# Three edits to an attention and two-MLP kernel: an operand in PSUM, planner slack for weight sums, a shorter attention stretch

## The chip, the cores and the metric

The kernel runs on one core of a Trainium2 chip. Five queues work side by side there: PE (matrix products into eight PSUM banks), DVE (VectorE), ACT (ScalarE), POOL (GpSimd) and SP, which here only issues DMAs. The metric is the device time of one execution in microseconds; lower is better.

## The reference

Windowed attention (4 batches, 8 heads, 576 positions, head size 64), then a gated MLP (width 1536), then an MLP (width 2048), over 2304 tokens of width 512, in fp32:

```python
scores = np.where((rel >= 0) & (rel < 128), q @ k.T / 8 + bias, -1e9)     # per head
attn = softmax(scores) @ v                                               # x: 2304 x 512
g, val = x @ w_gate, x @ w_val
x2 = (silu(g) * val) @ w_out                                             # first MLP
h = x2 @ moe2_w_in
out = silu(h) @ moe2_w_out                                               # second MLP
```

## The kernel before

**Tiles and parts.** The 2304 tokens are three parts of 768. A part is six tiles of 128 tokens, in two blocks of three (N = 384 columns). Each part goes through attention, the first MLP (`moe1`, six groups of 256 hidden units) and the second one (`moe2`, eight groups). PE does the MLPs without a break, first and second MLP of part 0, then part 1, then part 2; the attention of a part lies under the MLPs of the part before it. Inputs and weights are split into a high and a low fp32r half, and a product is three passes (high by high, high by low, low by high), at lines 902 to 904 for the way in (`quad`, seven Strassen products X, Y, Z over 2 x 2 blocks) and 1182 to 1184 or 1212 to 1214 for the way out (`out1`, `out2`).

**The operand of an MLP.** `operands` makes the seven Strassen operands of an input in `XOP`, slots 0 to 6. Its source is `XST` (from attention) or `ACC` (the first MLP's result). Slot 0 (A11) is block 0, columns 0 and 1 of the source. Slots 5, 6, 1 and 4 (S1, S2, S3, S4 and sums of them) come from differences t1 to t4 that `less` writes to PSUM banks. t1 is block 1 minus block 0, and t2 (slot 6, the S2 of the second product) needs t1. `split` writes the high half with a copy (`copy_op`, line 348 on ACT, 349 on DVE) and the low half with a subtraction (`sum_op`, line 357 on DVE, 358 on POOL). If the source is a PSUM bank, the subtraction can only go to DVE.

**The out-sums.** `out1` of group g adds PE's bank to ACC on DVE (line 1196) and gives the bank back. In the last group the block b = 0 comes last, columns d = 0, 1, 2, 3.

**Weight sums in the background.** Part 2 takes Strassen sums of the out-weights as well. `out_sums` makes them during part 1, in 11 jobs (one a group, where there is room): for each of two weights it loads the high half into `word` and the low half into the one buffer `top`, adds them (the word sum, 22 in all), forms four sums (`strassen_sums`, tiles `sums`), splits them (`split_weight`, tiles `later_raw`) and stores them. Part 2 loads them back into tiles `later_...`, some of which take the place of attention's buffers.

**What sets the order.** Every operation goes to a planner (`Plan.add`) with a cost for each engine that can do it, a due time, and what it reads and writes. `Plan.issue` then simulates the engines: an operation is ready when those before it end plus a hand-over time, and each engine takes, of those ready, the one with the earliest due time. This gives each engine a fixed list of instructions, which the chip executes strictly in that order. So an instruction that waits holds up all behind it in its list. `spread` gives attention's tiles their due times: over a stretch `span`, tile by tile. `WLEAD` is how far ahead weights are loaded. Out-weights go through a ring of three buffers `wo0` to `wo2`, two a group, so that the second load of a group waits until the group before has read its first weight for the last time.

Of the kernel before, what the change touches and what calls it, by code (L numbers as in the profile page):

```python
# [56 lines left out]
class Plan:  # L57
# [19 lines left out]
    def add(self, engine, cost, due, fn, reads=(), writes=(), take=None, give=None, port=False, other=()):  # L77
        n = len(self.ops)
        preds = set()
        for key in reads:  # L80
            if key in self.writer:
                preds.add(self.writer[key])
            self.readers.setdefault(key, []).append(n)
        for key in writes:
            if key in self.writer:
                preds.add(self.writer[key])
            preds.update(self.readers.pop(key, ()))
            self.writer[key] = n
        preds.discard(n)
        if isinstance(take, Bank):  # L90
            take = (take,)
        ways = {e: (c, f, p or e == "pool", d) for e, c, f, p, d in [(engine, cost, fn, port, 0.0), *other]}
        self.ops.append((ways, due, preds, take, give))

    def issue(self):
# [25 lines left out]
        def start(e, n, now):  # L121
            ways, _, _, take, _ = ops[n]
            if ways[e][2]:
                now = max(now, port_free)
            if take is not None:
                m = len(take)
                if len(self.banks) < m or any(used[k] + m > self.limits[k] for k in kinds(take[0])):
                    return None
                now = max(now, heapq.nsmallest(m, self.banks)[-1][0])
            if len(ways) > 1 and min(ways, key=lambda o: done(o, n)) != e:  # L130
                return None
            return now
# [27 lines left out]
        while left:  # L160
# [6 lines left out]
            ways, due, _, take, give = ops[n]  # L167
# [25 lines left out]
            for m in succs[n]:  # L193
                for o in ready_at[m]:
                    ready_at[m][o] = max(ready_at[m][o], end + handover(o, e))
                missing[m] -= 1
                if not missing[m]:
                    offer(m)
# [3 lines left out]
def attention_moe_moe2_kernel(  # L202
# [144 lines left out]
    def copy_op(n, due, out, src, reads, writes, give=None, psum=True):  # L347
# [4 lines left out]
            other=[("dve", cost("dve", n), dve, not psum, 500.0)],  # L352
        )

    def sum_op(n, due, out, x, y, op, reads, writes, give=None, psum=False):
# [5 lines left out]
        else:  # L361
            plan.add(
                "pool", cost("pool", n), due, pool, reads, writes, give=give,
                other=[("dve", cost("dve", n), dve, True, 500.0)],
# [309 lines left out]
    def operands(src, name, due, plain=True):  # L674
# [5 lines left out]
        def block(j, blk, kk):  # L680
            c = 2 * j + kk
            return (
                lambda: src[:, blk * BT:blk * BT + BT, c, :],
                [(name, blk * BT + t, c) for t in range(BT)],
            )
# [16 lines left out]
        for kk in range(2):  # L702
            t1[kk] = less(b[0, 1, kk], b[0, 0, kk])
# [58 lines left out]
    def split_weight(dst, key, src, reads, n, due, old=()):  # L762
        out = dst if callable(dst) else lambda: dst
        copy_op(n, due, lambda: out()[:, 0], lambda: src, reads, [key, *old], psum=False)
        sum_op(n, due, lambda: out()[:, 1], lambda: src, lambda: out()[:, 0].bitcast(F32), ALU.subtract, reads, [key])
# [22 lines left out]
    def strassen_sums(a, due):  # L788
        def add(x, y, op):
# [3 lines left out]
            sum_op(2 * P, due, lambda: t, lambda: xa, lambda: ya, op, xk + yk, [tk])  # L793
# [62 lines left out]
    def out_sums(kind, g, due, behind):  # L856
# [14 lines left out]
        for n, (t, tk) in enumerate(strassen_sums(a, due)):  # L871
            m = take("stage", len(STAGE))
            u, uk = STAGE[m][0], ("stage", m)
            split_weight(u, uk, t, tk, 2 * P, due, before.pop(uk, ()))
# [297 lines left out]

    def out1(g, ws, d, blk, hs, due):
# [19 lines left out]
        if g == 0:  # L1193
# [36 lines left out]
    WLEAD = 19050.0  # L1230
    pend = []
# [139 lines left out]
    spread(2, state["t"] + 6000.0, M1 + M2 - 8000.0)  # L1371
# [47 lines left out]
```

## Time and profile before

| | us |
|---|---|
| median of 3 runs | 941.37 |
| lowest, highest | 935.42, 941.68 |
| the profiled execution | 937.67 |
| its span, first to last instruction | 936.0 |
| PE busy in it | 907.9 |
| DVE, POOL, ACT busy | 708.9, 559.6, 531.0 |

All columns of the section of rows are in microseconds from the start of the span, or microseconds of duration, unless a mean is given in ns. In a timeline a row is start, duration, engine, line, instruction and tiles (written <- read), and in brackets the idle time of the engine ahead of it and what ended it. A group of instructions has its count, then busy us, mean ns, then idle time ahead and what ended it. Buffer numbers are left out of tile names. PE's durations are modelled and overlap: a matmul of 512 columns is shown with 0.39 us where the next starts 0.23 us later.

### The profile page before, as it was taken

Reading aid. Unit: us, or ns where it says so; the run is one execution under the profiler, and the core shown is the slowest. Engines: PE = TensorE matmul, PEld = TensorE weight load, DVE = VectorE, ACT = ScalarE, POOL = GpSimd, SP = SyncE. Lnnn points to the kernel's source line nnn. Section 1 sums busy time; section 2 is a strip of 40 time slices with the busy share of each in tenths; the row PEclk is TensorE's granted clock in tenths of the full one; section 3 lists DMA queues with packets and bytes.
Section 4 is the critical chain, followed back from the end, with each engine's and each line's share of the span. In section 5 each row is a group of like instructions: output and inputs, shape, how many; then the busy total and the mean of one; then the engine's idle time right before and its main releaser. Section 6 shows DMA issues by size and latency. Waiting matters only on the chain.

```text
span 936.0 us, 17803 instructions
## 1 busy us (share of the span) xinstructions
PE 907.9 (97%) x5758; PEld 843.8 (90%) x5758; DVE 708.9 (76%) x1602; ACT 531.0 (57%) x1361; POOL 559.6 (60%) x635
## 2 busy tenths in 40 slices
PE   7999999998999999999999999999999999999998
PEld 5799999997888888989999988888799999999996
DVE  7888879879889788647565867667755776778875
ACT  6887567757877675664343575445355333474431
POOL 2865468777657678785524487754144445876453
PEclk9999999999999999999999999999999999999999
DMA  9988997996897987999877789988498888678702
GB/s 222 281 243 258 283 324 221 294 313 206 274 304 260 305 290 265 354 314 304 279 219 244 242 292 330 312 284 311 151 329 249 251 253 253 201 234 245 218 23 91
DMA packets 181677, 241.58 MB, mean 258 GB/s; under 512 B 68048, under 2 KB 97232, under 8 KB 181584
## 3 DMA queue, kind: packets, MB, share of 16 engines
q1 hardware_dynamic: 181584, 240.44, 80.0%
q8 instruction: 46, 0.75, 0.3%
q14 instruction: 47, 0.39, 0.1%
HBM read 169.61 MB, written 70.78 MB: 257 GB/s over the span
## 4 chain that ended last, share of the span: by engine, by line
PE 69%; DVE 12%; DMA 7%; POOL 4%; ACT 4%; issue 3%; SPq 0%; DVEq 0%; POOLq 0%; ACTq 0%
PE bank L902 13%; PE bank L904 12%; PE bank L903 12%; PE bank L1212 4%; PE bank L1214 4%; PE bank L1213 4%; PE bank L607 3%; PE bank L493 3%; PE bank L1182 2%; PE bank L1184 2%; PE bank L1183 2%; DVE word L755 2%; DMA top<-kept_o 2%; PE bank L1118 1%; PE bank L1120 1%
## 5 line engine op out<-in xcount | busy, mean ns | idle before, releaser
L902 PE MATMUL bank<-XOP,wu 128*128 128x384 f32 (+1 forms) x868 | 297.3, 343 | 11.6 <-DVE tmp L963 4.3
L903 PE MATMUL bank<-XOP,wu 128*128 128x384 f32 (+1 forms) x868 | 288.9, 333 | 2.5 <-POOL XOP L358 1.9
L904 PE MATMUL bank<-XOP,wu 128*128 128x384 f32 (+1 forms) x868 | 288.9, 333 | 0.0
L902 PEld LDWEIGHTS bank<-XOP,wu 128*128 128x128 f32 x868 | 163.1, 188 | 23.0 <-ACT tmp L348 8.2
L903 PEld LDWEIGHTS bank<-XOP,wu 128*128 128x128 f32 x868 | 163.3, 188 | 4.4 <-POOL XOP L358 2.1
L904 PEld LDWEIGHTS bank<-XOP,wu 128*128 128x128 f32 x868 | 163.0, 188 | 0.1
L358 POOL TENSOR_TENSOR h<-tmp,h 128x384 fp32r<-128x384 f32 x77 | 81.7, 1071 | 62.0 <-ACT h L348 60.9
L348 ACT ACTIVATE tmp<-bank 128x384 f32<-128x384 f32 x133 | 62.1, 488 | 52.8 <-PE bank L904 28.2
L1026 DVE SCALAR_TENSOR_TENSOR tmp<-tmp,bank 128x384 f32<-128x384 f32 (+1 forms) x120 | 64.4, 542 | 36.4 <-ACT tmp L1015 24.4
L1212 PE MATMUL bank<-wo,h 128*128 128x512 f32 (+1 forms) x218 | 87.3, 401 | 1.7 <-DMA wo<-kept_o 1.7
L1214 PE MATMUL bank<-wo,h 128*128 128x512 f32 (+1 forms) x218 | 85.6, 393 | 0.0
L1213 PE MATMUL bank<-wo,h 128*128 128x512 f32 (+1 forms) x218 | 85.6, 393 | 0.0
L553 POOL TENSOR_TENSOR cs<-cs,st 128x512 f32<-128x512 f32 x36 | 39.9, 1109 | 65.8 <-DVE st L550 44.7
L1224 DVE TENSOR_TENSOR ACC<-bank,ACC 128x512 f32<-128x512 f32 (+1 forms) x97 | 64.1, 678 | 15.4 <-PE bank L1214 14.6
L358 POOL TENSOR_TENSOR wu<-word,wu 128x256 fp32r<-128x256 f32 x63 | 51.1, 824 | 39.4 <-ACT wu L348 35.2
L348 ACT ACTIVATE h<-tmp 128x384 fp32r<-128x384 f32 x97 | 49.5, 523 | 41.9 <-PE bank L1213 20.0
L1182 PE MATMUL bank<-h,wo 128*128 128x384 f32 (+1 forms) x216 | 72.5, 336 | 0.1
L1183 PE MATMUL bank<-h,wo 128*128 128x384 f32 (+1 forms) x216 | 71.5, 331 | 0.1
L1184 PE MATMUL bank<-h,wo 128*128 128x384 f32 (+1 forms) x216 | 71.4, 330 | 0.0
L1015 ACT ACTIVATE tmp<-bank 128x384 f32<-128x384 f32 (+1 forms) x121 | 57.0, 482 | 25.0 <-PE bank L904 11.5
L755 DVE SCALAR_TENSOR_TENSOR word<-raw,top 128x512 int32<-128x512 int32 x68 | 60.9, 895 | 11.7 <-ACT top L752 9.6
L948 DVE TENSOR_TENSOR bank<-bank,tmp 128x384 f32<-128x384 f32 x93 | 52.1, 561 | 22.1 <-PE bank L904 20.3
(414 smaller groups left out, 2149.6 us busy)
## 6 DMA issues: line engine op xcount, KB each, us to landing
wu<-kept_i SPq DMA_DIRECT2D x112, 256.0 KB, 3.5
wu<-kept_g SPq DMA_DIRECT2D x72, 256.0 KB, 4.2
wu<-kept_v SPq DMA_DIRECT2D x72, 256.0 KB, 4.3
wo<-kept_o SPq DMA_DIRECT2D x34, 512.0 KB, 4.7
raw<-in_moe_w_out_dram SPq DMA_DIRECT2D x28, 512.0 KB, 4.9
kept_o<-wo SPq DMA_DIRECT2D x28, 512.0 KB, 4.4
kept_i<-wu SPq DMA_DIRECT2D x56, 256.0 KB, 4.5
kept_s<-later_raw SPq DMA_DIRECT2D x44, 256.0 KB, 4.8
```

The lines of the kernel that those rows point to most:

```text
L348: act = lambda: nc.scalar.activation(out(), src(), AF.Copy)
L358: pool = lambda: nc.gpsimd.tensor_tensor(out(), x(), y(), op)
L755: lambda: nc.vector.scalar_tensor_tensor(w.bitcast(I32), word, 13, top, ALU.logical_shift_right, ALU.bitwise_or),
L902: nc.tensor.matmul(ps, wh, xh, start=start, stop=False, skip_group_check=True)
L903: nc.tensor.matmul(ps, wh, xl, start=False, stop=False, skip_group_check=True)
L904: nc.tensor.matmul(ps, wl, xh, start=False, stop=stop, skip_group_check=True)
L1182: nc.tensor.matmul(ps[:, 0:n], wh, h[:, 0], start=(i == 0), stop=False)
L1183: nc.tensor.matmul(ps[:, 0:n], wh, h[:, 1], start=False, stop=False)
L1184: nc.tensor.matmul(ps[:, 0:n], wl, h[:, 0], start=False, stop=(i == 1))
L1212: nc.tensor.matmul(ps, hh, wh, start=(i == 0), stop=False)
L1213: nc.tensor.matmul(ps, hh, wl, start=False, stop=False)
L1214: nc.tensor.matmul(ps, hl, wh, start=False, stop=(i == 1))
```

## The change

There are three edits.

1. **The operand.** Where the last group of `out1` sums block 0, columns 0 and 1, the sum is written back to PE's own bank (line 1200 of the changed kernel) instead of ACC, and the bank is kept (`left`). In `operands` with source ACC, slot 0 and t1 read this bank. t1 waits until slot 0 is split (`x_keys(0, kk)`), and gives the bank back.
2. **The slack.** `Plan.add` takes a `slack`, which is added to the time at which an operation counts as ready. The background sums and their splits get LATE = 4000 ns each; the word sums get none.
3. **The stretch.** The attention of part 2 is spread over M1 + M2 - 28000 ns instead of M1 + M2 - 8000.

```diff
-    def add(self, engine, cost, due, fn, reads=(), writes=(), take=None, give=None, port=False, other=()):
+    def add(self, engine, cost, due, fn, reads=(), writes=(), take=None, give=None, port=False, other=(), slack=0.0):
...
-                    ready_at[m][o] = max(ready_at[m][o], end + handover(o, e))
+                    ready_at[m][o] = max(ready_at[m][o], end + handover(o, e) + ops[m][5])
...
             c = 2 * j + kk
+            if src is ACC and j == 0 and blk == 0:
+                return (lambda b=left[kk]: tiles(b.tile[:, 0:N])), [left[kk]]
...
         for kk in range(2):
-            t1[kk] = less(b[0, 1, kk], b[0, 0, kk])
+            held = src is ACC
+            t1[kk] = less(b[0, 1, kk], b[0, 0, kk], x_keys(0, kk) if held else (), left[kk] if held else None)
...
-        for n, (t, tk) in enumerate(strassen_sums(a, due)):
+        for n, (t, tk) in enumerate(strassen_sums(a, due, LATE)):
             m = take("stage", len(STAGE))
             u, uk = STAGE[m][0], ("stage", m)
-            split_weight(u, uk, t, tk, 2 * P, due, before.pop(uk, ()))
+            split_weight(u, uk, t, tk, 2 * P, due, before.pop(uk, ()), LATE)
...
-        if g == 0:
+        if g == G1 - 1 and b0 == 0 and d < 2:
+            plan.add("dve", cost("dve", n), due, lambda: nc.vector.tensor_tensor(pv(), pv(), acc, ALU.add), keys, [b])
+            left[d] = b
+        elif g == 0:
             copy_op(n, due, lambda: acc, pv, [b], keys, give=b)
...
+    LATE = 4000.0
...
-    spread(2, state["t"] + 6000.0, M1 + M2 - 8000.0)
+    spread(2, state["t"] + 6000.0, M1 + M2 - 28000.0)
```

The rest of the diff hands `slack` through `copy_op`, `sum_op`, `split_weight` and `strassen_sums`. All lists of instructions are planned anew, from the first edit's place in part 0 on. In all, PE's list is as long as before; 19 of the 22 word sums stand on DVE (14 before), and the six low halves of slot 0 in the three hand-overs from ACC stand on DVE instead of POOL.

**DVE, hand-over from ACC in part 0.** L1196 is an out-sum, L693 (L695) a difference t, L357 with XOP a low half. Before, from the out-sum of block 0, column 0 on:

```order
L1196 TENSOR_TENSOR ACC_65<-bank4_132,ACC_65 128x3x128
L357 TENSOR_TENSOR XOP_63<-bank1_129,XOP_63 128x384
L1196 TENSOR_TENSOR ACC_65<-bank6_134,ACC_65 128x3x128
L1196 TENSOR_TENSOR ACC_65<-bank7_135,ACC_65 128x3x128
L1196 TENSOR_TENSOR ACC_65<-bank5_133,ACC_65 128x3x128
L693 TENSOR_TENSOR bank2_130<-ACC_65 128x384
L693 TENSOR_TENSOR bank4_132<-ACC_65,bank2_130 128x384
L448 TENSOR_TENSOR KR_66<-bank3_131,KR_66 128x2x128
L693 TENSOR_TENSOR bank7_135<-ACC_65 128x384
L357 TENSOR_TENSOR XOP_63<-bank4_132,XOP_63 128x384
L693 TENSOR_TENSOR bank5_133<-ACC_65,bank7_135 128x384
L357 TENSOR_TENSOR XOP_63<-bank2_130,XOP_63 128x384
```

After, from the same sum (now L1200) on:

```order
L1200 TENSOR_TENSOR bank4_132<-bank4_132,ACC_65 128x384
L357 TENSOR_TENSOR XOP_63<-bank1_129,XOP_63 128x384
L1200 TENSOR_TENSOR bank6_134<-bank6_134,ACC_65 128x384
L357 TENSOR_TENSOR XOP_63<-bank4_132,XOP_63 128x384
L695 TENSOR_TENSOR bank2_130<-ACC_65,bank4_132 128x384
L357 TENSOR_TENSOR XOP_63<-bank6_134,XOP_63 128x384
L695 TENSOR_TENSOR bank4_132<-ACC_65,bank2_130 128x384
L758 SCALAR_TENSOR_TENSOR word2_98<-raw1_94,top0_95 128x512
L1205 TENSOR_TENSOR ACC_65<-bank7_135,ACC_65 128x3x128
L357 TENSOR_TENSOR XOP_63<-bank4_132,XOP_63 128x384
L695 TENSOR_TENSOR bank7_135<-ACC_65,bank6_134 128x384
L357 TENSOR_TENSOR XOP_63<-bank2_130,XOP_63 128x384
```

The low halves of slot 0 (XOP<-bank4 and XOP<-bank6, third and fifth behind the sum) are new here. The first low half of slot 6 (the second XOP<-bank4) is ninth behind the sum in both lists. A weight conversion (L758, L755 before) has come ahead of it.

**ACT and DVE, first background sum, at the end of part 0's second MLP.** On ACT L1015 (L1018) is a tanh, and L348 with later_raw the high half of a background sum. ACT before:

```order
L348 ACTIVATE tmp2_108<-bank6_134 128x384
L348 ACTIVATE tmp3_109<-bank4_132 128x384
L348 ACTIVATE tmp4_110<-bank5_133 128x384
L348 ACTIVATE KR_66<-bank1_129 128x2x128
L348 ACTIVATE later_raw0_256_4727<-sums_99 128x256
L1015 ACTIVATE tmp2_108<-bank6_134 128x384
L348 ACTIVATE later_raw0_256_4727<-sums_99 128x256
L456 ACTIVATE qts_119<-bank3_131 128x256
L348 ACTIVATE later_raw1_256_4746<-sums_99 128x256
L1015 ACTIVATE tmp4_110<-tmp5_111 128x384
```

ACT after:

```order
L348 ACTIVATE tmp2_108<-bank2_130 128x384
L348 ACTIVATE XST_64<-bank3_131 128x512
L456 ACTIVATE qts_119<-bank4_132 128x256
L348 ACTIVATE KR_66<-bank0_128 128x2x128
L348 ACTIVATE tmp3_109<-bank7_135 128x384
L348 ACTIVATE tmp4_110<-bank5_133 128x384
L456 ACTIVATE qts_119<-bank6_134 128x256
L1018 ACTIVATE tmp2_108<-bank2_130 128x384
L1018 ACTIVATE tmp4_110<-tmp5_111 128x384
L1018 ACTIVATE tmp3_109<-bank5_133 128x384
L1018 ACTIVATE tmp5_111<-bank7_135 128x384
L348 ACTIVATE later_raw1_256_4797<-sums_99 128x256
```

The four tanhs stand ahead of the first high half of a background sum now. On DVE, L948 (L951) adds to Y, L963 (L966) is the c22 that frees Y's bank. Before, the job's second word sum was on POOL, and DVE had:

```order
L948 TENSOR_TENSOR bank4_132<-bank4_132,tmp2_108 128x384
L448 TENSOR_TENSOR KR_66<-bank1_129,KR_66 128x2x128
L1026 SCALAR_TENSOR_TENSOR tmp2_108<-tmp2_108,bank6_134 128x384
L963 TENSOR_TENSOR tmp5_111<-bank4_132,tmp4_110 128x384
L459 SCALAR_TENSOR_TENSOR qts_119<-bank3_131,qts_119 128x256
L948 TENSOR_TENSOR bank5_133<-bank5_133,tmp3_109 128x384
```

After:

```order
L448 TENSOR_TENSOR KR_66<-bank1_129,KR_66 128x2x128
L357 TENSOR_TENSOR word0_96<-word0_96,top0_95 128x512
L459 SCALAR_TENSOR_TENSOR qts_119<-bank4_132,qts_119 128x256
L951 TENSOR_TENSOR bank7_135<-bank7_135,tmp2_108 128x384
L448 TENSOR_TENSOR KR_66<-bank0_128,KR_66 128x2x128
L459 SCALAR_TENSOR_TENSOR qts_119<-bank6_134,qts_119 128x256
L1029 SCALAR_TENSOR_TENSOR tmp2_108<-tmp2_108,bank2_130 128x384
L966 TENSOR_TENSOR tmp5_111<-bank7_135,tmp4_110 128x384
```

The second word sum (word0) has come to DVE, ahead of the additions to Y.

**PE, last out-products of part 1's second MLP.** Of the three passes of a product only the first is shown. From the last product of the group before with wo1 on, before:

```order
L1212 MATMUL bank7_135<-wo1_91,h4_104 128x512
...
L1212 MATMUL bank7_135<-wo2_92,h1_101 128x512
...
L1212 MATMUL bank4_132<-wo0_90,h3_103 128x512
...
L1212 MATMUL bank0_128<-wo0_90,h3_103 128x512
...
L1212 MATMUL bank5_133<-wo0_90,h3_103 128x512
...
L1212 MATMUL bank6_134<-wo0_90,h2_102 128x512
...
L1212 MATMUL bank7_135<-wo0_90,h2_102 128x512
...
L1212 MATMUL bank4_132<-wo1_91,h4_104 128x512
```

After:

```order
L1221 MATMUL bank2_130<-wo1_91,h4_104 128x512
...
L1221 MATMUL bank2_130<-wo2_92,h1_101 128x512
...
L1221 MATMUL bank0_128<-wo0_90,h3_103 128x512
...
L1221 MATMUL bank1_129<-wo0_90,h3_103 128x512
...
L1221 MATMUL bank7_135<-wo0_90,h3_103 128x512
...
L1221 MATMUL bank6_134<-wo0_90,h2_102 128x512
...
L1221 MATMUL bank3_131<-wo0_90,h2_102 128x512
...
L1221 MATMUL bank4_132<-wo0_90,h2_102 128x512
...
L1221 MATMUL bank0_128<-wo1_91,h4_104 128x512
```

Between the last product with the old wo1 and the first with the new one stand 18 matmuls before and 21 after. The weighing of the last attention tile (L607), which stood directly ahead of the first row, is now 75 rows ahead of it.

## Rows read from the trace of the kernel before

**Rows 1.** Page, part 1: busy us (share of span) x instructions.
```profile
PE 907.9 (97%) x5758; PEld 843.8 (90%) x5758; DVE 708.9 (76%) x1602; ACT 531.0 (57%) x1361; POOL 559.6 (60%) x635
```

**Rows 2.** Windows: stretch, length, busy us (x instructions) by engine, clock, DMA share, GB/s.
```profile
220.00:230.00 10.00, 8.36 (x46) 7.54 (x47) 9.78 (x20) 6.87 (x18) 6.39 (x8) 1.00 0.32 77
```

**Rows 3.** Timeline of PE: rows with idle time ahead, two neighbours at 669.
```profile
220.16 0.45 PE L903 MATMUL bank<-XOP,wu 128*128 128x384 f32 x1 [1.87 <-POOL XOP L358]
...
226.79 0.44 PE L902 MATMUL bank<-XOP,wu 128*128 128x384 f32 x1 [0.75 <-ACT tmp L348]
228.83 0.44 PE L902 MATMUL bank<-XOP,wu 128*128 128x384 f32 x1 [0.73 <-DVE tmp L349]
...
419.50 0.44 PE L902 MATMUL bank<-XOP,wu 128*128 128x384 f32 x1 [1.92 <-DVE tmp L963]
...
464.39 0.44 PE L902 MATMUL bank<-XOP,wu 128*128 128x384 f32 x1 [0.24 <-DVE tmp L963]
...
514.80 0.44 PE L902 MATMUL bank<-XOP,wu 128*128 128x384 f32 x1 [0.70 <-ACT tmp L348]
...
539.10 0.44 PE L902 MATMUL bank<-XOP,wu 128*128 128x384 f32 x1 [0.80 <-ACT tmp L348]
...
634.24 0.45 PE L902 MATMUL bank<-XOP,wu 128*128 128x384 f32 x1 [0.42 <-ACT tmp L348]
...
669.06 0.39 PE L1213 MATMUL bank<-wo,h 128*128 128x512 f32 x1
669.29 0.40 PE L1214 MATMUL bank<-wo,h 128*128 128x512 f32 x1
671.42 0.47 PE L1212 MATMUL bank<-wo,h 128*128 128x512 f32 x1 [1.73 <-DMA wo<-kept_o]
```

**Rows 4.** Timelines of DVE and POOL, hand-over from ACC in part 0.
```profile
217.31 1.47 DVE L1196 TENSOR_TENSOR ACC<-bank,ACC 128x384 f32<-128x384 f32 x3
...
220.10 1.40 DVE L693 TENSOR_TENSOR bank<-ACC 128x384 f32<-128x384 f32 x1
...
217.80 6.52 POOL L358 TENSOR_TENSOR XOP<-ACC,XOP 128x384 fp32r<-128x384 f32 x6
```

**Rows 5.** Groups by line and form: busy us, mean ns, idle; L755 from the page.
```profile
L357 DVE TENSOR_TENSOR XOP<-bank,XOP 128x384 fp32r<-128x384 f32 x48 | 25.3, 549 | 0.7 <-ACT XOP L348 0.3
L358 POOL TENSOR_TENSOR XOP<-ACC,XOP 128x384 fp32r<-128x384 f32 x18 | 19.3, 1107 | 1.1 <-ACT XOP L348 1.1
L357 DVE TENSOR_TENSOR word<-word,top 128x512 f32<-128x512 f32 x14 | 12.0, 860 | 27.0 <-DMA top<-kept_o 19.0 <-DMA word<-kept_o 7.2 <-POOL h L358 0.7
L693 DVE TENSOR_TENSOR bank<-ACC 128x384 f32<-128x384 f32 x12 | 9.1, 759 | 0.1
L693 DVE TENSOR_TENSOR bank<-ACC,bank 128x384 f32<-128x384 f32 x12 | 6.7, 554 | 0.2
L755 DVE SCALAR_TENSOR_TENSOR word<-raw,top 128x512 int32<-128x512 int32 x68 | 60.9, 895 | 11.7 <-ACT top L752 9.6
```

**Rows 6.** Timelines of POOL, ACT, DVE: what stood before PE's 419.50.
```profile
415.46 1.30 POOL L358 TENSOR_TENSOR word<-word,top 128x512 f32<-128x512 f32 x1 [2.05 <-DMA word<-kept_o]
...
417.60 0.42 ACT L348 ACTIVATE later_raw<-sums 128x256 fp32r<-128x256 f32 x1 [2.11 <-POOL sums L358]
417.92 0.47 ACT L1015 ACTIVATE tmp<-bank 128x384 f32<-128x384 f32 x1
...
418.90 0.55 DVE L963 TENSOR_TENSOR tmp<-bank,tmp 128x384 f32<-128x384 f32 x1
```

**Rows 7.** Waits over the kernel: total us, times, longest us.
```profile
ACT later_raw L348 <- POOL sums L358: 26.0, 10, 8.2
```

**Rows 8.** The chain that ended last, in order: start, us, what.
```profile
408.14 7.18 DMA word<-kept_o
...
665.52 5.76 DMA wo<-kept_o
```

**Rows 9.** Page, part 6: DMA issues, KB each, median us to landing.
```profile
wo<-kept_o SPq DMA_DIRECT2D x34, 512.0 KB, 4.7
```

## What I predict, and how

> **What bounds the kernel now.** I read the page's busy shares first: TensorE (PE) is busy for 907.9 of 936.0 us [rows 1], at the full granted clock of 2.4 GHz, also in a slice in which it waits [rows 2]. So PE is the bound, its matmuls are untouched by the change, and the change can only be worth what PE waits. Next I went through the slices of 10 us: the startup apart, PE is short of work where the operand of one MLP is turned into the next one's (220 to 230) and where a weight sum was late (410 to 420). Then I took PE's timeline, kept the rows with idle time ahead of them, and looked at what ended each. [Rows 3] holds the larger waits in the stretches that the change touches. Three families are seen there:
>
> - The operand of the second MLP (ACC to XOP), in part 0 at 220.16, 226.79 and 228.83 and in part 1 at 539.10: 1.87 + 0.75 + 0.73 + 0.80 = 4.15 us.
> - Background weight sums at 419.50, 464.39, 514.80 and 634.24: 1.92 + 0.24 + 0.70 + 0.42 = 3.28 us.
> - A weight load, at 671.42: 1.73 us.
>
> These idle times count from a modelled end. By starts, the wait at 671.42 is 2.13 us after the matmul at 669.29, where neighbours start 0.23 us apart (669.06, 669.29): 1.90 us, so each wait costs about 0.17 us more than its row says. All nine together: 9.16 + 9 x 0.17 = 10.7 us, 1.1% of the span. That is nearly all that is to be had from these three edits.
>
> **The operand kept in PSUM.** At each of three hand-overs (one a part) two sums go to PSUM instead of ACC, as long as before. The high halves are then read from PSUM by ScalarE. The two low halves per hand-over move from POOL, 1107 ns each, to VectorE (DVE), 549 ns each; and the two differences t1 have one operand in SBUF instead of two, 554 ns for 759 ns [rows 5]. On DVE that is 2 x 0.55 - 2 x 0.21 = +0.7 us per hand-over; POOL is relieved of 2.2 us.
>
> In part 0 POOL took six low halves in a row, 217.80 to 224.32 [rows 4], and PE's second matmul waited for the second of them, until 220.16. After the change the sum ends, as before, near 216.9 (in [rows 4] the next sums start at 217.31). ScalarE needs 0.5 us and the low half stands third behind the sum on DVE; with DVE's instructions 0.47 us apart (three in 1.47 us, [rows 4]) it ends near 218.4. The first wait shrinks from 1.87 us to about 0.2. But PE then reaches S2 some 1.6 us earlier, and the low half of S2 stands at the same place as before, nine rows behind the sum. Before, it followed a subtraction from two SBUF operands that took 1.40 us at 220.10 while POOL ran [rows 4], and so ended near 222.0. Now I count rows to about 221.3: PE has its products with A11 done by 220.4 and waits some 0.9 us, and about as much again for the second half of S2, since a weight conversion (L755, 895 ns in the mean, [rows 5]) has moved ahead of each. So nearly all of the 1.7 us is lost again within ten products. What remains is that DVE gets to the additions of Y earlier, on which 226.79 and 228.83 hang: half of their 1.48 us. I take -0.9 us for part 0, from -3.4 (all three waits go) to +2.0 (two low halves and two conversions, 2 x 0.55 + 2 x 0.9 = 2.9 us of DVE work ahead of S2, less the 0.85 that the slow subtraction lost against its 0.55). In parts 1 and 2 the first matmuls did not wait for A11, so there is only 0.80 us to win and 0.7 us of DVE work each to pay: -0.4, from -0.8 to +1.4. Sum of this edit: **-1.3**.
>
> The banks held longer cost nothing that I can find: each waits for a split that takes about 1.5 us, while PE works on out-sums of other banks.
>
> **The slack.** The wait at 419.50 can be followed in [rows 6]: a word sum waited on POOL for a load that took 7.18 us [rows 8]; then came the Strassen sums, and ScalarE stood at 417.60 before a high half of such a sum. Right behind it in the same queue was the tanh for PE's next bank (417.92), then DVE's c22 (418.90), then PE. Over the kernel ScalarE stood so for 26.0 us [rows 7]. With 4 us added to every step the planner puts these instructions behind the tanhs, as the order of ScalarE shows. But the word sum itself has no slack and now stands on DVE, right ahead of the work on Y. That queue waits for the same load, until 408.14 + 7.18 = 415.32 [rows 8]. From there: 0.86 for the sum (mean, [rows 5]); then two instructions of 384 columns at 0.47 and three of 256, by width 0.31; then c22, 0.55: 418.6 against 419.45 (418.90 + 0.55, [rows 6]). The first wait shrinks by 0.8 only. The other three (1.36 + 3 x 0.17 = 1.9) stand behind sums and halves that are delayed, and I let 1.8 of it go. Against this, 19 of the 22 word sums are now on DVE instead of 14; 14 of them had 27.0 us of idle time before them [rows 5], 1.9 each, so DVE idles about 10 us more. Little of such idle time reached PE so far (the 0.24 at 464.39 is the clear case), so +0.4. Sum: **-2.2**, from -4.0 to +5 (if half of those 10 us reached PE).
>
> **The shorter stretch.** The same attention work of the last part is done by 20 us earlier (28000 for 8000 ns off the span). It adds no instruction. PE did not wait for its result: at 676 there is no wait in the operand of part 2. But it changes the order at the end of part 1. There wo1 is loaded when its last reader is through, at 665.52, and lands 5.76 us later [rows 8]; PE had 18 matmuls of 0.23 us to do meanwhile and stood 1.73 us. The change leaves 21: 0.7 us. The 34 such loads land in 4.7 us in the median [rows 9], 1.1 less than this one. With 0.7 + half of 1.1: **-1.2**, from -1.9 (all) to +1 (the load now stands in SP's queue behind a store of the last weight sums, which the slack has made later).
>
> **Sum.** -1.3 - 2.2 - 1.2 = -4.7 us. The profiled execution took 937.67 us: 933.0. It lies 3.7 us under the median of the three runs (941.37) and 2.3 over the lowest, so the runs of one kernel differ by as much as I forecast.
>
> **A rule weighed against the rows.** In [rows 5] the subtraction with two SBUF operands takes 759 ns, that with one 554: 0.2 us lost to POOL's presence. The Trainium skill, SBUF — State Buffer, section Who interferes with whom, says that a VectorE instruction with two SBUF inputs and a GpSimd instruction that reads SBUF exclude each other for a whole instruction, and that one with at most one SBUF input doesn't. The 1.40 us at 220.10 agrees. By the rule the six t1 would escape up to one GpSimd instruction each, an estimate of 6 x 1.1 = 6.6 us of DVE's time by the durations here; if the two in part 0 stood on PE's path, the sum would be 931.2 for 933.0. By the rows it is 6 x 0.2 = 1.2 us, which the +0.7 per hand-over above holds already, and I keep to that. Another rule speaks against the change: by the Trainium skill, PSUM — Partial Sum Buffer, section The four PSUM rules, GpSimd cannot touch PSUM at all, so that the planner has no way to give these low halves back to POOL. No trace here can show it; what it does to the time is rival 2.
>
> **Rivals.**
>
> 1. Every wait named goes: 937.67 - 10.7 = 927.0. For it: each has one visible cause. Against it: the row counts for S2 and for the word sum above.
> 2. The low halves, which POOL no longer takes, make DVE late at each hand-over: part 0 at +2.0, parts 1 and 2 together at +1.4, the other terms halved (-1.7): 939.4. For it: DVE is busy for 9.78 of the 10 us from 220 to 230 [rows 2] and has hardly a gap to take more work into. This is also the time if the new order only trades waits. It decides once S2 is later than 222.8 in part 0.
> 3. Slower: DVE, standing for loads with the bank work behind it, hands its idle time to PE. Half of 10 us more from five sums, and as much from the 27.0 us already there as sums move closer to bank work: 937.67 + 5 + 5 - 2.5 (the other two edits) = 945.2. It decides where a load lands over 1.5 us after DVE has reached its sum. Against it: in the trace PE has several banks ahead of DVE at most sums.
>
> **How the numbers follow.** Forecast 0.52 (930 to 937), rival 1 0.15, rival 2 0.22, rival 3 0.11. The range of 926 to 943 leaves out about a third of rival 1 and most of rival 3, under 0.2. One per cent, about what a measurement of this kernel can tell from no change, is 9.4 us at the median of 941.37: under 932.0 or over 950.8. Under 932.0 lie rival 1 and a third of the forecast: 0.15 + 0.17 = 0.32. Over 950.8 lies the worse half of rival 3: 0.05. Within: 0.63.
>
> **What would show it.** After the change, right: PE's first wait in part 0 near 218 under 0.5 us, and a new one before S2 or S1 (DVE XOP L357) of about 1 us; at 417 to 419 under 1.3 us; ScalarE's wait for POOL's sums under 10 us of the 26.0; at the end of part 1 under 1 us for wo. Wrong: DVE's wait for loads of top over 45 us with PE rows that end on c22 or Y behind it; a wait for wo that stays at 1.7 us or more; part 0's hand-over without a second wait.

## The result, and the profile after

The changed kernel took 932.04 us in the median of 10 runs (927.36 to 934.46), the kernel before 939.67 in the median of its 10 (935.42 to 941.68). The ratio is 0.9914, with a 95% interval of 0.9893 to 0.9934: 8.1 us less, from 6.2 to 10.1 (the two medians alone differ by 7.6). The forecast was 933.0 and its sum 4.7 us. So the direction and the range held, and the gain was larger than the sum.

PE's busy time on the page, the line that answers [rows 1]:

```profile
PE 908.2 (97%) x5758; PEld 843.9 (91%) x5758; DVE 703.4 (75%) x1598; ACT 530.4 (57%) x1363; POOL 557.4 (60%) x637
```

PE's timeline of the changed kernel, the rows that answer [rows 3]:

```profile
219.41 0.44 PE L906 MATMUL bank<-XOP,wu 128*128 128x384 f32 x1 [0.42 <-DVE XOP L357]
...
223.66 0.41 PE L905 MATMUL bank<-XOP,wu 128*128 128x384 f32 x1 [1.40 <-ACT XOP L348]
...
226.63 0.45 PE L906 MATMUL bank<-XOP,wu 128*128 128x384 f32 x1 [0.15 <-DVE XOP L357]
...
418.11 0.44 PE L905 MATMUL bank<-XOP,wu 128*128 128x384 f32 x1 [0.86 <-ACT tmp L348]
...
438.60 0.44 PE L905 MATMUL bank<-XOP,wu 128*128 128x384 f32 x1 [0.17 <-DVE tmp L966]
...
475.01 0.44 PE L905 MATMUL bank<-XOP,wu 128*128 128x384 f32 x1 [0.34 <-DVE tmp L966]
...
527.53 0.44 PE L1188 MATMUL bank<-h,wo 128*128 128x384 f32 x1 [1.17 <-DVE KR L448]
...
540.74 0.44 PE L905 MATMUL bank<-XOP,wu 128*128 128x384 f32 x1 [0.60 <-ACT tmp L348]
...
667.73 0.40 PE L1223 MATMUL bank<-wo,h 128*128 128x512 f32 x1
668.27 0.47 PE L1221 MATMUL bank<-wo,h 128*128 128x512 f32 x1
```

The promised signs are there. The first wait of part 0 is 0.42 for 1.87. A new one of 1.40 stands before S2. At 418.11 there is 0.86 for 1.92. At 668.27, where wo1 is first read, the matmul starts 0.54 us after the one ahead of it, against 2.13 before. ScalarE's wait for POOL's background sums, 26.0 us in [rows 7], has no row any more. One larger wait is new and was not foreseen: 527.53.

Two rows show how a background word sum still reaches PE. DVE and ACT ahead of 418.11, then DVE ahead of 527.53:

```profile
415.80 0.87 DVE L357 TENSOR_TENSOR word<-word,top 128x512 f32<-128x512 f32 x1 [4.27 <-DMA word<-kept_o]
...
416.92 0.55 DVE L951 TENSOR_TENSOR bank<-bank,tmp 128x384 f32<-128x384 f32 x1
```

```profile
417.57 0.87 ACT L348 ACTIVATE tmp<-bank 128x384 f32<-128x384 f32 x2 [2.25 <-DVE bank L951]
```

```profile
526.43 0.71 DVE L357 TENSOR_TENSOR word<-word,top 128x512 f32<-128x512 f32 x1 [1.42 <-DMA top<-kept_o]
527.07 0.41 DVE L448 TENSOR_TENSOR KR<-bank,KR 128x256 fp32r<-128x256 f32 x1
```

At 415.80 DVE had stood 4.27 us for a load, with the addition to Y behind it, ScalarE's copy behind that, and PE at 418.11. At 526.43 it had stood 1.42 us, with KR (the low half of attention's keys) behind, on which PE's 527.53 waited. The word sums are the one step of the background work that got no slack.

The groups by form that answer [rows 5]:

```profile
L357 DVE TENSOR_TENSOR XOP<-bank,XOP 128x384 fp32r<-128x384 f32 x54 | 28.4, 549 | 1.0 <-ACT XOP L348 1.0
L358 POOL TENSOR_TENSOR XOP<-ACC,XOP 128x384 fp32r<-128x384 f32 x12 | 12.3, 1037 | 4.5 <-ACT XOP L348 4.5
L695 DVE TENSOR_TENSOR bank<-ACC,bank 128x384 f32<-128x384 f32 x18 | 9.8, 556 | 0.2
L695 DVE TENSOR_TENSOR bank<-ACC 128x384 f32<-128x384 f32 x6 | 4.4, 742 | 0.0
```

Six low halves have come to DVE at the 549 ns that the sum used, and six differences read one operand from PSUM, at 556 ns. The 759 ns that the sum set against this is the mean of all twelve differences with two operands in ACC. The six that changed took 0.89 us each before: 0.56 and 1.40 us in part 0, 1.44 and 0.56 in part 1, 0.61 and 0.78 in part 2.

### The profile page after: what moved, and what is told of

Read it like the earlier page. It is cut to its first block, busy times and chain, and to the rows that moved or that the text cites. A ratio compares the mean times of both kernels' runs of the same rounds, so it can differ in the third digit from the quotient of the medians.

```text
span 932.3 us, 17799 instructions
## 1 busy us (share of the span) xinstructions
PE 908.2 (97%) x5758; PEld 843.9 (91%) x5758; DVE 703.4 (75%) x1598; ACT 530.4 (57%) x1363; POOL 557.4 (60%) x637
## 4 chain that ended last, share of the span: by engine, by line
PE 68%; DVE 11%; DMA 7%; POOL 7%; ACT 3%; issue 3%; SPq 0%; DVEq 0%; POOLq 0%; ACTq 0%
PE bank L905 12%; PE bank L906 12%; PE bank L907 12%; PE bank L1221 5%; PE bank L1223 5%; PE bank L1222 5%; PE bank L493 3%; PE bank L607 3%; PE bank L1188 2%; PE bank L1190 2%; PE bank L1189 2%; DMA raw<-in_moe_w_in_dram 2%; DMA top<-kept_o 2%; DVE word L758 1%; POOL h L358 1%
## 5 line engine op out<-in xcount | busy, mean ns | idle before, releaser
L358 POOL TENSOR_TENSOR h<-tmp,h 128x384 fp32r<-128x384 f32 x81 | 86.0, 1073 | 81.7 <-ACT h L348 69.5
L348 ACT ACTIVATE tmp<-bank 128x384 f32<-128x384 f32 x135 | 62.9, 488 | 73.0 <-PE bank L907 43.0
L348 ACT ACTIVATE h<-tmp 128x384 fp32r<-128x384 f32 x96 | 49.1, 522 | 50.4 <-PE bank L1222 25.1
L951 DVE TENSOR_TENSOR bank<-bank,tmp 128x384 f32<-128x384 f32 x93 | 52.3, 563 | 27.4 <-PE bank L907 23.9
L1018 ACT ACTIVATE tmp<-bank 128x384 f32<-128x384 f32 (+1 forms) x121 | 57.1, 482 | 21.7 <-DVE bank L951 9.7
L758 DVE SCALAR_TENSOR_TENSOR word<-raw,top 128x512 int32<-128x512 int32 x68 | 59.7, 877 | 12.8 <-ACT top L755 11.5
```

The source lines that it names most:

```text
L348: act = lambda: nc.scalar.activation(out(), src(), AF.Copy)
L358: pool = lambda: nc.gpsimd.tensor_tensor(out(), x(), y(), op)
L758: lambda: nc.vector.scalar_tensor_tensor(w.bitcast(I32), word, 13, top, ALU.logical_shift_right, ALU.bitwise_or),
```

## The experiments

The table has all twelve runs beside the two kernels. "us" is the ratio's distance from 1 times 939.4, with its 95% interval. "Loads" is the time for which DVE and POOL stood before a word sum for the load of `word` or `top`, from each kernel's waits. "Part 0" is the length of part 0's second MLP and "part 1" that of part 1's two MLPs in the profiled execution, from PE's timeline, between the starts of the last out-products of the stages (before: 217.56 to 368.87, and 368.87 to 676.16). These lengths are of one execution each: those of e1 and e2 took 941.51 and 942.69 us, 5.9 and 3.6 above the medians of their kernels, with a granted clock of 0.99 in part 1.

| kernel | ratio | us | loads: DVE / POOL | part 0 | part 1 |
|---|---|---|---|---|---|
| before | 1 | | 26.2 / 13.1 | 151.3 | 307.3 |
| changed | 0.9914 | -8.1 (-10.1 to -6.2) | 19.2 / 1.9 | 149.9 | 304.3 |
| r1_after, the same again | 0.9909 | -8.5 (-10.8 to -6.3) | 24.4 / 0.6 | 148.1 | 304.3 |
| e1_psum_only | 0.9971 | -2.7 (-4.7 to -0.7) | 22.0 / 12.0 | 149.1 | 312.1 |
| e2_slack_only | 0.9995 | -0.5 (-3.4 to +2.5) | 18.8 / 32.6 | 150.7 | 311.6 |
| e3_stretch_only | 0.9991 | -0.8 (-2.6 to +1.0) | 27.0 / 17.9 | 151.2 | 308.1 |
| d1_no_psum | 0.9936 | -6.0 (-8.1 to -3.9) | 25.3 / 0 | 150.8 | 303.4 |
| d2_no_slack | 0.9958 | -3.9 (-6.2 to -1.7) | 17.1 / 13.0 | 148.4 | 309.9 |
| d3_no_stretch | 0.9899 | -9.5 (-12.0 to -7.0) | 18.5 / 27.5 | 147.7 | 306.3 |
| g1_word_slack | 0.9869 | -12.3 (-15.1 to -9.6) | 0 / 3.8 | 148.6 | 299.5 |
| g2_stretch48 | 0.9878 | -11.5 (-14.0 to -8.8) | 17.4 / 31.9 | 148.1 | 301.0 |
| h2_all_slack_only | 0.9921 | -7.4 (-9.6 to -5.2) | 0 / 4.4 | 150.7 | 301.1 |
| h3_word_stretch48 | 0.9870 | -12.2 (-14.8 to -9.6) | 0 / 4.4 | 147.6 | 300.3 |
| h4_words_only_slack | 0.9882 | -11.1 (-13.4 to -8.7) | 0 / 1.3 | 149.1 | 301.3 |

All diffs are against the changed kernel. My theory was the sum of the prediction; the rivals were that one edit carries all, or that the edits work only together.

**One edit alone.** In e1_psum_only the slack and the stretch are undone:

```diff
-    LATE = 4000.0
+    LATE = 0.0
...
-    spread(2, state["t"] + 6000.0, M1 + M2 - 28000.0)
+    spread(2, state["t"] + 6000.0, M1 + M2 - 8000.0)
```

> Only the operand in PSUM; no slack, and the attention of the last part over the long stretch. Theory (the three edits add up as my terms did): 1.3 us less than before; PE's first wait in part 0 near 218 under 0.5 us and a new wait of about 1 us before S2; the weight-sum wait near 419 stays at 1 to 2 us, and the wo wait at the end of part 1 stays (18 matmuls under the load, as before: 1 to 2 us if the load takes over 5 us). Rival A (one edit carries the whole gain, and it is this one): 6 us or more less than before. Rival B (the operand costs DVE time at the hand-over): 1 to 4 us more than before, with waits between 217 and 235 that together exceed the 3.35 us of before.

Measured: 2.7 us less, twice the term of 1.3, which lies in the interval. Rivals A and B fall. The wo wait stayed, at 1.57 us, and so did the one near 419, at 2.09.

In e2_slack_only the operand and the stretch are undone, in e3_stretch_only the operand and the slack. The operand is undone so:

```diff
-            if src is ACC and j == 0 and blk == 0:
+            if False:
...
-            held = src is ACC
+            held = False
...
-        if g == G1 - 1 and b0 == 0 and d < 2:
+        if False:
```

> Only the slack of 4000 ns for the background sums and their halves. Theory (terms add up): 2.2 us less than before; the waits of before at 419.50, 514.80 and 634.24 go to under 1.3 in all, ScalarE's wait for POOL's sums falls from 26.0 us to under 10, and the wo wait at the end of part 1 stays, since 18 matmuls still lie under the load. Rival A (the slack carries nearly all, since a queue that does not stand for a late load no longer hands the load's scatter to PE): 5 to 8 us less than before in the medians, although the named waits are worth only 3.3. Rival B (the slack alone only moves the waits): within 1 us of before, with new waits of PE of the same size at other weight sums.

> Only the shorter stretch for the last part's attention. My term as it stands on record: 1.2 us less than before, out of the wo wait at the end of part 1. Against it speaks the order of PE in this kernel: with the stretch alone still 18 matmuls lie under that load (21 only together with the slack). Theory now (the wo wait goes by the number of matmuls): the wo wait stays at 0.5 to 2 us by how long the load takes, and the time is within 1 us of before. Rival (the stretch brings the gain by another way: less attention work beside the last out-products): 2 to 4 us less than before, with fewer PE waits in 640 to 680.

Measured: the slack alone brought next to nothing (rival B). Its trace shows new waits in place of the old. POOL and PE of the slack-only kernel at the first job, then DVE and PE at a later one:

```profile
418.86 1.28 POOL L358 TENSOR_TENSOR word<-word,top 128x512 f32<-128x512 f32 x1 [3.39 <-DMA word<-kept_o]
...
421.78 0.63 POOL L584 TENSOR_SCALAR_AFFINE_SELECT u<-u 128x512 f32<-128x512 f32 x1
```

```profile
422.47 0.44 PE L607 MATMUL bank<-u,vld 128*64 128x128 f32 x4 [2.36 <-POOL u L584]
```

```profile
587.14 0.96 DVE L357 TENSOR_TENSOR word<-word,top 128x512 f32<-128x512 f32 x1 [1.99 <-DMA word<-kept_o]
588.02 0.54 DVE L966 TENSOR_TENSOR tmp<-bank,tmp 128x384 f32<-128x384 f32 x1
```

```profile
588.62 0.45 PE L905 MATMUL bank<-XOP,wu 128*128 128x384 f32 x1 [1.15 <-DVE tmp L966]
```

Both times a word sum stands for its load at the head of a queue: ahead of the masks of the last part's attention (L584), and ahead of a c22 (L966). The planner's own rule says why. In `issue` a load of 256 KB counts as landed 1.1 + 0.73 + 0.9 = 2.7 us after its issue if it goes alone. On the chip these loads land after 4.7 (top) and 5.1 us (word) in the median of the kernel before. A word sum without slack stands some 2 us too early.

The stretch alone is within 1 us of before, as the theory of that expectation said. But that theory put the wo wait down to 18 matmuls, and with 18 there was no wait at all. SyncE's queue of the kernel before and of the stretch-only kernel shows the reason:

```profile
663.80 1.39 SPq L891 DMA_DIRECT2D later_l<-kept_o  x2
665.52 0.33 SPq L772 DMA_DIRECT2D wo<-kept_o  x1
665.90 0.90 SPq L891 DMA_DIRECT2D later_u<-kept_s  x2
```

```profile
647.89 1.43 SPq L894 DMA_DIRECT2D later_l<-kept_o  x2
649.36 1.07 SPq L894 DMA_DIRECT2D later_u<-kept_s  x2
...
668.17 1.02 SPq L775 DMA_DIRECT2D wo<-kept_o  x2
```

Before, four loads of part 2's weights go out around the load of wo1. They go into buffers of the last part's attention (l, u) and wait until it is through. With the shorter stretch they have gone some 16 us earlier, and the wo load is alone but for the next one. The four kernels with the long stretch and 18 matmuls (before, e1, e2, d3) wait 1.4 to 1.9 us there; the load lands 5.5 to 5.9 us after its issue. The five with a shorter one and 18 (e3, d2, g1, h3, h4) wait 0 to 0.14, and it lands after 3.2 to 4.2 us. In h2, with the long stretch and 21 matmuls, there was no wait either, but its load landed after 4.7 us, so what the three more matmuls are worth by themselves isn't shown. In d1 (below) the four loads stand around an earlier load of wo, which lands after 6.9 us, and the wait comes there:

```profile
649.34 0.50 PE L1221 MATMUL bank<-wo,h 128*128 128x512 f32 x1 [1.34 <-DMA wo<-kept_o]
```

**One edit taken away.** In d1_no_psum the operand is undone, in d2_no_slack the slack, in d3_no_stretch the stretch, each as above.

> The changed kernel without the operand in PSUM: slack and stretch together. Terms of the record: 3.4 us less than before, 1.3 more than the changed kernel. Theory now (slack and stretch act together: only with both do 21 matmuls lie under the wo load): most of the gain is here, 5 to 8 us less than before; the wo wait under 0.5 us, the wait near 419 under 1.3, and the hand-over in part 0 as before with its first wait of 1.5 to 2 us. Rival (the operand carries the gain): within 2 us of before.

> The changed kernel without the slack: operand in PSUM and shorter stretch. Terms of the record added: 2.5 us less than before. The singles measured so far (operand 2.7 less, stretch 0.9 less) would add up to 3.6 less. Theory now (slack and stretch only work together, since either alone leaves sums in the queues of ScalarE or DVE in part 1's second MLP, 530 to 676, and 18 matmuls under the wo load): 2 to 4 us less than before, 4 us or more over the changed kernel; that stage as long as in the stretch-only kernel (about 148 us from its first to its last out-product, against 141 in the changed kernel). Rival (the operand and the stretch are the pair that matters): within 2 us of the changed kernel.

> The changed kernel without the shorter stretch: operand in PSUM and slack. Terms of the record added: 3.5 us less than before. The singles measured so far (operand 2.7 less, slack 0.5 less) would add up to 3.2 less. Theory now (slack and stretch only work together): 2 to 4 us less than before, 4 us or more over the changed kernel, the stage from 530 to 676 about 148 us long, with a wo wait that goes by its load. Rival (operand and slack are the pair that matters): within 2 us of the changed kernel.

Measured: slack and stretch give 6.0 us together (d1), where each alone gave under 1. That spoke for the theory that they need each other. d3 refutes it: operand and slack without the stretch are as fast as the changed kernel. With the slack, the operand alone or the stretch alone is enough. My reading is that the slack needs a plan in which its word sums don't meet something urgent. d2, without the slack, is 4 us behind, as expected. d3 doesn't fit this reading well. It still has the three waits of the slack-only kernel, two of them shorter and one longer: 1.32 for 2.36 us (POOL's L584), 1.42 for 1.89 (wo) and 1.58 for 1.15 (DVE's L966). PE's idle time in part 1 is 6.5 us, against 7.9 in the slack-only kernel and 6.7 in the kernel before. Why d3 is 9 us faster than the slack-only kernel is only partly explained: the operand is worth some 2.7 of it, the clock (below) some 2. The rest is open.

**The word sums.** g1_word_slack gives them the slack too, g2_stretch48 shortens the stretch further instead.

```diff
-            sum_op(KC * P, due, lambda w=w: w, lambda w=w: w, lambda low=low: low, ALU.add, ["top"], [wk])
+            sum_op(KC * P, due, lambda w=w: w, lambda w=w: w, lambda low=low: low, ALU.add, ["top"], [wk], slack=LATE)
```

```diff
-    spread(2, state["t"] + 6000.0, M1 + M2 - 28000.0)
+    spread(2, state["t"] + 6000.0, M1 + M2 - 48000.0)
```

> The changed kernel with 4000 ns of slack on the word sums too. By my step on record, a word sum without slack stands ahead of PE's banks and hands its wait for a load to PE; then this version gains: DVE's wait for loads of word and top falls from 19 us to under 8, the wait at 418 goes, 1 to 2 us less than the changed kernel. Theory now: those waits of DVE lie in time that nobody on PE's path needs, so nothing is won there, and the sums come later still. It has 18 matmuls under the last wo load of part 1, like before, for 21: if that number carries the gain of slack and stretch, it is 2 to 5 us slower than the changed kernel with a wo wait of up to 2 us; if it does not, the time is within 1 us of the changed kernel.

> The changed kernel with the last part's attention over a stretch shorter by another 20 us (48000 ns off the span). It keeps the 21 matmuls under the wo load. Theory (attention out of the way of sums in part 1's second MLP is what the stretch brings): what is left to gain there is the waits of 640 to 680, under 0.8 us, so it is within 1.5 us of the changed kernel, either way, with more waits of PE in part 1's first MLP (376 to 530), where the attention work now stands. Rival (the more the better): another 2 us or more less. Rival (attention then crowds the first MLP of part 1): 2 us or more over the changed kernel.

Measured: g1 gains some 4 us on the changed kernel, and my "nothing is won there" was wrong. Of the waits of word sums for loads, one is left:

```profile
POOL word L358 <- DMA top<-kept_o: 3.8, 1, 3.8
```

The waits of 418.11 and 527.53 are gone, PE's idle time in part 1 is 1.0 us for 3.8, and part 1 is 4.8 us shorter, all of it with 18 matmuls under the wo load. g2 is as fast (the rival "the more the better"), though its word sums wait 49 us; PE stands idle for only 1.6 us in its part 1. Little that is urgent seems to stand behind these sums with the attention 20 us further ahead, but no run shows that as the reason.

**Which slack.** The changed kernel was run again beside three versions. h2_all_slack_only is g1 with operand and stretch undone, h3_word_stretch48 is g1 and g2 in one, and h4_words_only_slack has the slack on the word sums alone:

```diff
-        for n, (t, tk) in enumerate(strassen_sums(a, due, LATE)):
+        for n, (t, tk) in enumerate(strassen_sums(a, due)):
...
-            split_weight(u, uk, t, tk, 2 * P, due, before.pop(uk, ()), LATE)
+            split_weight(u, uk, t, tk, 2 * P, due, before.pop(uk, ()))
```

> The changed kernel itself, beside the three versions that follow on the same chip. Expected: the ratio of before, 0.9914, again within 0.003; PE's wait at 418 about 0.9 us, the hand-over of part 0 as in the trace after the change.

> The kernel before with 4000 ns of slack on all background steps, the word sums too; the operand and the stretch as before. Theory (the word sums without slack spoilt the slack-only kernel: on POOL one held the last part's masks until PE's wait of 2.4 us at 422, on DVE one held a c22 until PE's wait at 589): both waits go, 4 to 6 us less than before where the slack-only kernel gained 0.5. Rival (slack needs the shorter stretch or the operand, whichever steps have it): within 2 us of before, with waits over 1 us left between 400 and 640.

> The changed kernel with slack on the word sums and the stretch shorter by another 20 us, both of which were faster than the changed kernel by about 4 us. Theory (both take away the same waits, those in part 1, which came to about 4.5 us in the changed kernel): no more than 1 us less than the better of the two, so 4 to 6 us less than the changed kernel. Rival (they act on different waits): 7 us or more less than the changed kernel.

> The changed kernel with the slack on the word sums alone; the Strassen sums and their halves have none. Theory (a queue is held by whatever instruction of this work comes first in it, and the sums and halves inherit the delay of their word): the halves again stand ahead of tanhs, ScalarE's wait for POOL's sums is over 15 us again, and the time is 2 to 4 us over the changed kernel. Rival (the loads are what is late, and only the word sums meet them): as fast as the version with slack on all steps, 4 us less than the changed kernel, with ScalarE's wait for POOL's sums under 10 us.

Measured: the changed kernel came out as before (0.9909), though its wait near 418 was 0.47 us, not 0.9, and PE's first wait in part 0 was gone. h2 gains 7.4 us without the other two edits, where the same slack without the word sums gained 0.5; both waits of the slack-only kernel are gone. h3 is no faster than g1 or g2, so as far as the time tells these take away the same waits. h4 refuted its theory: its time is that of g1, and ScalarE waits little for POOL's sums though these have no slack. Its waits:

```profile
ACT later_raw L348 <- POOL sums L358: 6.5, 8, 1.8
...
POOL word L358 <- DMA top<-kept_o: 1.3, 1, 1.3
```

What was late were the loads, and only word sums meet loads. Put in the right place, they leave the sums and halves behind them on time. So the change's slack sits on the wrong steps: h2 against the slack-only kernel shows it clearly, h4 against the changed kernel by 2 to 3 us, with intervals that overlap. It isn't the only way, since g2 and d3 do as well or nearly without it. Nor does any run show how far the time moves when only the plan is made anew; every version here has its lists planned anew, and 4000 ns is the only slack that was run. The versions with slack on the word sums beat the changed kernel: g1 took 927.25 us in the median, h3 927.14, h4 928.29, each beside 939.4 of before.

## Why the prediction was right, and where it was not

**The bound and the signs** held: PE's busy time stayed (908.2 for 907.9 us) and waits changed, most of them at the places named.

**The operand: -1.3 forecast, 2.7 us less alone.** The pattern came as worked out, with other sizes and one other cause. The first low half ended 1.4 us after the sum (1.5 worked out). The second wait was 1.40 instead of 0.9, and it was not for the low half of S2. DVE, changed kernel, and the same wait of PE in g2:

```profile
222.50 0.55 DVE L357 TENSOR_TENSOR XOP<-bank,XOP 128x384 fp32r<-128x384 f32 x1
222.96 0.56 DVE L695 TENSOR_TENSOR bank<-ACC,bank 128x384 f32<-128x384 f32 x1
```

```profile
220.04 0.41 PE L905 MATMUL bank<-XOP,wu 128*128 128x384 f32 x1 [1.32 <-DVE bank L695]
```

The low half was ready at 223.05, and PE began at 223.66, 0.14 us after the second difference t1 had ended (223.52). That difference gives back the bank in which the second column of A11 was kept, and in the changed kernel's list the product with S2 writes this bank. In the list before, it wrote one that attention had given back. All nine profiles of kernels with the operand have this wait (1.28 to 1.40 us). In each it ends 0.14 to 0.15 us behind that difference and 0.6 behind the low half, and in d2, g1 and g2 the row names the difference. (The row at 223.66 names a copy of ScalarE for another operand, which ended in the same moment.) So the step "the banks held longer cost nothing that I can find" failed: the held bank cost about 0.5 us here, an estimate from these rows.

In this profile a load came in as well:

```profile
218.81 0.54 DVE L357 TENSOR_TENSOR XOP<-bank,XOP 128x384 fp32r<-128x384 f32 x1
...
220.50 0.56 DVE L357 TENSOR_TENSOR XOP<-bank,XOP 128x384 fp32r<-128x384 f32 x1 [0.68 <-ACT XOP L348]
```

```profile
219.34 0.80 ACT L755 ACTIVATE top<-raw 128x512 f16<-128x512 bf16 x1 [0.85 <-DMA raw<-in_moe_w_in_dram]
220.01 0.46 ACT L348 ACTIVATE XOP<-bank 128x384 fp32r<-128x384 f32 x1
```

ScalarE took a weight conversion that waited for its load ahead of the second high half, and DVE lost 0.68 us: a wait for a load that I had not counted. It didn't make the second wait longer: in r1, d2, g1 and g2, where ScalarE didn't stand for that load, the wait was 1.29 to 1.32. On the other side the wait for the second half of S2 was 0.15 instead of about 0.9, and the waits of 226.79 and 228.83 went wholly, where I let half. From 217 to 235 the idle time fell by 1.2 us (3.35 to 2.19), near the forecast of 0.9.

The term was too small all the same: all nine profiles with the operand have a part 0 shorter than all five without (148.5 against 150.9 in the mean, 2.4 us). Some 1.5 us of that lie in the first 17.5 us of the stage (PE idle for 1.85 us in the mean against 3.31). Another 0.9 lie in the 42 us behind, where kernels without the operand have small waits (before: 0.55 us at 274.13, behind a c22) and those with it have hardly any (0.06 us in the mean against 0.93). I had looked at the hand-over only. Whether the later part comes from the 2.2 us less on POOL isn't shown. In part 1, 0.80 became 0.60.

The differences t1 saved more than the sum had: 6 x (890 - 556) = 2.0 us of DVE, not 6 x 0.2 = 1.2, since 759 was a mean over others too. The Trainium skill, SBUF — State Buffer, section Who interferes with whom, says that a VectorE instruction with two SBUF inputs contends with a GpSimd instruction that reads SBUF. The estimate of up to 6.6 us that the prediction worked out from it isn't reached: two of the six took 1.40 and 1.44 us, the others 0.56 to 0.78.

**The slack: -2.2 forecast.** The step on 419.50 was right: the word sum without slack keeps about half of that wait (1.1 us left by the prediction, 0.86 measured), though PE stood behind the addition to Y and ScalarE's copy, not behind c22. The three other waits went or shrank: 0.34 at 475.01 and 0.17 at 438.60 are left of 1.36. The 0.4 for word sums on DVE became 1.17, at 527.53. Wrong was the step that five more word sums on DVE bring 10 us more of idle time there: DVE's waits for these loads fell from 26.2 to 19.2 us, POOL's from 13.1 to 1.9. And I took the slack as a term of its own. Alone it is worth 0.5 us; whether it pays seems to hang on what stands behind the word sums, which the other two edits decide.

**The stretch: -1.2 forecast, 1.6 of the wo wait gone.** The size of that wait was right and the reason was not: the loads beside it rather than the matmuls under it. As a term of the sum it isn't borne out: the stretch alone gave 0.8 us (within the noise), and the changed kernel without it (d3) was no slower.

**The sum.** Part 0 became 1.4 and 3.2 us shorter in the two profiles of the changed kernel and part 1 3.0 in both, where the terms had 0.9 and 3.8. The sum was made against one execution, which had the full clock throughout (1.000) and lay 2.0 us under the later median of 939.67; that 933.0 came so near 932.04 is luck in part. Over the runs the mean granted clock was 0.9965 in 29 runs of the kernel before and 0.9986 in ten of the changed one. Over 936 us that difference is 2.0 us (an estimate: PE is the bound, so what the clock loses is time). It isn't sure: single runs of g1 and d2 have a mean of 0.949 and 0.952, and yet took 925.66 us (the fastest of g1) and 937.69 (the median of d2 is 937.13). With it, and 1.4 us more for the operand, the 4.7 becomes 8.1. That the figures meet so well is partly chance: the 2.7 us of the operand alone hold some clock already (0.9973 in those runs), and the stretch up to 217, which no edit touches, alone took from 214.8 to 220.2 us in the profiled executions.

**The rivals.** None came as told. Every wait going (927.0) is nearly what g1 and h3 reach. Rival 2 met its sign in the changed kernel's profile (S2 at 223.66, later than 222.8, where the stage began 0.6 us later), and yet part 0 became shorter, so the sign didn't decide. Waits for loads reaching PE (rival 3) is the mechanism at 418.11 and 527.53 and in the slack-only kernel, but as a smaller gain and not as a loss.

## What to carry to other kernels

Where a fixed order is planned with loads that land later than planned, try the slack on the one step that waits for the load, not on the steps behind it; here slack on all steps gave 7.4 us, and the same slack without the word sums 0.5. A bank that is kept longer has a price if the next product takes it: look up which product does. Before costing a move, list what stands in the queue behind each instruction that waits for a DMA, since that decides the price. A wait for a load may go by the transfers issued beside it, and what frees their buffers.

## What was not expected of the hardware

After some long waits PE ran at its lower clock for a few microseconds, so that a wait cost more than its row. PE's timeline of the slack-only kernel at the wo wait, and the windows behind it (busy us by engine, granted clock, DMA share, GB/s):

```profile
675.35 0.47 PE L1221 MATMUL bank<-wo,h 128*128 128x512 f32 x1 [1.89 <-DMA wo<-kept_o]
675.66 0.39 PE L1222 MATMUL bank<-wo,h 128*128 128x512 f32 x1
...
676.61 0.63 PE L1222 MATMUL bank<-wo,h 128*128 128x512 f32 x1
677.04 0.63 PE L1223 MATMUL bank<-wo,h 128*128 128x512 f32 x1
```

```profile
676.00:679.20 3.20, 3.20 (x10) 2.42 (x9) 2.93 (x7) 1.17 (x3) 0.00 (x0) 0.51 0.33 125
```

The granted clock is 0.51, the level of 1.2 GHz, and matmuls start 0.43 us apart instead of 0.23. In these 3.2 us PE lost about 1.6, nearly as much as by the wait of 1.89. In the operand-only kernel the same followed a wait of 2.78 us at 636.89 (0.50 from 636 to 640). At the same place in the kernel before, after 1.73 us [rows 3], the clock stayed at 1.00.
